# The planner of a fused attention, MoE and soft-MoE kernel: earlier ready times for first products, and new counted matmul durations

## The chip, the core and the metric

One core of one Trainium2 chip runs the kernel. The metric is the device time of one execution in microseconds (us); smaller is better. The engines are TensorE (PE, with its weight loads as PEld), VectorE (DVE), ScalarE (ACT), GpSimd (POOL) and SyncE (SP, which issues the DMAs).

## What is computed

Attention with pooled keys and values, then a feed-forward pair with h·cos(h), then eight experts over all tokens, weighted by a matrix that is normalised by rows and columns eight times:

```python
def _moe_ref(x, w_in, w_out):                      # 2304 tokens, 512 -> 2048 -> 512
    h = x @ w_in
    return (h * np.cos(h)) @ w_out

def _moe2_ref(x, w_gate, w1, w2):                  # 8 experts, 512 -> 1024 -> 512
    ...
    for e in range(E):
        h = np.maximum(x @ w1[e], 0.0)
        out += P[:, e:e + 1] * (h @ w2[e])
    return out.astype(np.float32)
```

## The kernel before, in words

All matrix products are of fp32r halves: each operand is cut into a high and a low part, and three matmuls stand for one product (high·high, high·low, low·high). The experts' stage, from about 500 us to the end, is 16 units (8 experts, two halves of the hidden width) by 3 pairs of 384-token blocks: 48 steps. In each step two layers are multiplied by a seven-product scheme (P1 to P7, taken in the order P1 P5 P6 P2 P7 P3 P4). `first_layer` does it twice (h = 0, 1), in matmuls of 384 columns, six to a product: P1 goes into PSUM tile px1, ACT copies it into tile py, P5 goes into pv5, P6 is added into py, P2 into px1, P7 into py, P3 into pv5, P4 into py. `strassen_layer` does it for three row blocks i, in matmuls of 256 columns, six to a product. A PSUM tile p (trace name pc) and a tile q (qc) each hold 512 columns, in two halves p0, p1, q0, q1. Products come in pairs of twelve matmuls, one node of the planner each: P1 into p0 and P5 into p1; P6 into q0 and P2 into p0; P7 into q0 and P3 into p1; last P4 alone into q0. Between them ACT copies p0 to q0 and p1 to s5 (trace name t), DVE adds q0 and s5 into p1 and later s5 into q1 (trace: qc<-qc,t), and `accumulate` (L1550) adds p and q into the output.

Weights of a unit come in as tiles raw (or raw2 for the second layer); DVE or POOL combine them (raw<-raw,raw, 128x2x256), ACT makes the high half (whi, vhi), DVE or POOL the low half (wlo, vlo). `VG` gives such an operation to whichever of the two the planner finds earlier.

The order of the work on each engine is set by a planner, `Graph.schedule`. Every piece of work is a node with an engine and a duration (`mm` counts those of PE). `latest` (L207) walks back from the goals and gives each node a time `late` that ranks it. `schedule` keeps a clock for each engine and picks the ready node that can start within a short hold of the earliest and has the smallest `late`. When a node has run, its followers get their ready time:

```python
s.est = max(s.est, end + (0.35 * lap if same else self.SIGNAL[e] + s.pad))
```

`pad` is an extra of the follower, 0.0 unless set. The planner's times set the order alone; the waits that the built program has come from the tiles which an instruction reads and writes. Each engine then runs its own list in order. The line numbers of the profile are those of the code below.

Of the kernel before, what the change touches and what calls it, by code (L numbers as in the profile page):

```python
# [15 lines left out]
ALU = mybir.AluOpType  # L16
# [26 lines left out]
HD = DM // 2  # L43
# [109 lines left out]
class Graph:  # L153
# [19 lines left out]
    def buf(self, kind, shape, dtype, name):  # L173
        return Buf(kind, shape, dtype, name)
# [4 lines left out]
    def add(self, engine, us, run, reads=(), writes=(), port=False, table=None, size=0, goal=FAR, name=None, pad=0.0, release=0.0):  # L179
        node = Node()  # L180
        node.engine, node.us = (engine, us) if isinstance(engine, tuple) else ((engine,), (us,))
        node.run, node.port, node.table, node.size, node.goal = run, port, table, size, goal
        node.succ, node.new, node.bufs, node.done, node.est, node.name = [], [], [], False, release, name
        node.pad, node.spare, node.lap = pad, None, self.lap
        deps = set()
        for items, write in ((reads, False), (writes, True)):
            for item in items:
                buf, part = item if isinstance(item, tuple) else (item, None)
                if buf.kind and not buf.acc:
                    assert write, (name, buf.name)  # L190
                    node.new.append(buf)
                for other, its, wrote in buf.acc:
                    if other is not node and (write or wrote) and (part is None or its is None or part == its):
                        deps.add(other)
                buf.acc.append((node, part, write))
                if buf not in node.bufs:
                    node.bufs.append(buf)
                    buf.left += 1
                    if buf.kind:
                        for group in buf.kind.groups:  # L200
                            group.users += 1
        node.wait = len(deps)
        for other in deps:
            other.succ.append(node)
        self.nodes.append(node)
        return node

    def latest(self):
        for node in reversed(self.nodes):
            late = node.goal  # L210
            for s in node.succ:
                late = min(late, s.late - max(node.us) - self.SIGNAL[node.engine[0]])
            node.late = late
            if node.size:
                node.late -= 3.0 if node.engine == ("SP",) else 7.0
# [195 lines left out]
def two(n):  # L411
    return (n + 151) / 960
# [16 lines left out]


def mm(count, n):
    return count * {384: 0.1736, 256: 0.117, 512: 0.2325}[n]


def V(n, port=True):
    return {"engine": "V", "us": two(n), "port": port}
# [12 lines left out]
def fused_kernel(ctx: ExitStack, tc: tile.TileContext, qT, kT, kS, vS, v0, k1, v1, wa1, wb1, wa2, wb2, wg, out):  # L449
# [12 lines left out]
    late = g.group("late", "right", (early, turn), ahead)  # L462
# [75 lines left out]
    def activate(n, out, in_, func=AF.Copy, reads=(), writes=(), from_psum=False, table=None, us=None, goal=FAR, **more):  # L538
        return add("A", us or (actp if from_psum else act)(n),
                   lambda: nc.scalar.activation(out=out(), in_=in_(), func=func,  # L540
                                                **{k: v() if callable(v) else v for k, v in more.items()}),
                   reads, writes, table=table)
# [11 lines left out]
    def tt(how, out, in0, in1, op, reads, writes):  # L554

        def run(e=how["engine"]):
            (nc.gpsimd if e == "G" else nc.vector).tensor_tensor(out=out(), in0=in0(), in1=in1(), op=op)  # L557

        return add(how["engine"], how["us"], run, reads, writes, port=how.get("port", False))
# [13 lines left out]
    def pe(us, run, reads, writes, goal=None, pad=0.0, spare=None):  # L573

        if goal is None:
            goal = clock["t"]
            clock["t"] += us * clock["pace"]
        node = add("PE", us, run, reads, writes, goal=goal, pad=pad)
        node.spare = spare
        return node  # L580
# [412 lines left out]
    def hidden1(j, w, f, cut):  # L993

        hi, lo = xts[j]
        bank = buf(b_h, [P, 512], F32, "ph")
        ps = lambda: bank[:, :NB]
        wh, wl = w
        for part in ((0, 1), (2, 3)) if cut else ((0, 1, 2, 3),):
            pe(mm(3 * len(part), NB), lambda part=part: three(  # L1000
                ps(), NB, lambda c: (wh[:, c * P:(c + 1) * P], wl[:, c * P:(c + 1) * P]), lambda c: (hi[:, c, :], lo[:, c, :]),
                part, KC), [wh, wl] + [t.part(c) for t in (hi, lo) for c in part], [bank],
               spare=(lambda: bank[:, NB:]) if part[-1] == KC - 1 else None)
        return cosine(ps, bank)
# [529 lines left out]
    def accumulate(pair, u, j, i, po, acc2):  # L1534

        e = u // UE
        t = pair * 2 * TPB + j * TPB + i
        if j not in acc2:
            acc2[j] = buf(k_acc2[2 * pair + j], [P, TPB, DM], F32, "acc2")
        box = acc2[j]  # L1540
        a, pe_ = lambda: box[:, i, :], lambda: pr[:, t, e:e + 1]
        if e == 0:
            if u == 0:
                either(DM, a, lambda: po.tile, [po], [(box, i)])
            else:
                tt(V(DM, False), a, lambda: po.tile, a, ALU.add, [po], [(box, i)])
            if u == UE - 1:
                activate(DM, a, a, reads=[pr], writes=[(box, i)], scale=pe_)
        else:
            add("V", two(DM), lambda: nc.vector.scalar_tensor_tensor(  # L1550
                out=a(), in0=po.tile, scalar=pe_(), in1=a(), op0=ALU.mult, op1=ALU.add), [po, pr], [(box, i)])
        if u == NU - 1:
            load(lambda: out[t * P:(t + 1) * P, :], a, P * DM * 4, reads=[(box, i)])

    def strassen_layer(pair, u, pieces, w, acc2, goals, own=None):

        def mms(ps, name, i, start=False):
            r = slice(i * P, (i + 1) * P)
            for h in range(2):
                gh, gl = pieces[name, h]  # L1560
                k = slice(h * HD, (h + 1) * HD)
                for n, (l, m) in enumerate(((gh, w[name][0]), (gh, w[name][1]), (gl, w[name][0]))):
                    nc.tensor.matmul(out=ps, lhsT=l[:, r], rhs=m[:, k], start=(start and h + n == 0),  # L1563
                                     stop=(h + n == 3), skip_group_check=True)

        def needs(*names):
            return [t for n in names for h in range(2) for t in pieces[n, h]] + [t for n in names for t in w[n]]

        for i in range(TPB):
            kp, kq = (own or {}).get(i, (b_p, b_q))  # L1570
            p, q = buf(kp, [P, DM], F32, "pc"), buf(kq, [P, DM], F32, "qc")
            s5 = buf(k_t5, [P, HD], F32, "t5")
            p0, p1 = (lambda p=p: p[:, :HD]), (lambda p=p: p[:, HD:])
            q0, q1 = (lambda q=q: q[:, :HD]), (lambda q=q: q[:, HD:])

            def two_products(a, an, b, bn, start=False, i=i):
                def run():
                    mms(a(), an, i, start)
                    mms(b(), bn, i)
                return run  # L1580

            pe(mm(12, HD), two_products(p0, "P1", p1, "P5", True), needs("P1", "P5"), [p], goal=goals[i][0])
            activate(HD, q0, p0, reads=[p], writes=[q], from_psum=True)
            activate(HD, lambda s5=s5: s5.tile, p1, reads=[p], writes=[s5], from_psum=True)
            pe(mm(12, HD), two_products(q0, "P6", p0, "P2"), needs("P6", "P2"), [p, q], goal=goals[i][1])
            tt(V(HD, False), p1, q0, lambda s5=s5: s5.tile, ALU.add, [q, s5], [p])
            pe(mm(12, HD), two_products(q0, "P7", p1, "P3"), needs("P7", "P3"), [p, q], goal=goals[i][2])
            tt(V(HD, False), q1, q0, lambda s5=s5: s5.tile, ALU.add, [s5], [q])
            accumulate(pair, u, 0, i, p, acc2)
            pe(mm(6, HD), lambda i=i, q0=q0: mms(q0(), "P4", i), needs("P4"), [q], goal=goals[i][3])  # L1590
            accumulate(pair, u, 1, i, q, acc2)
# [103 lines left out]
```

## Time and profile before

| | us |
|---|---|
| device time, median of 3 runs (lowest, highest) | 1903.47 (1903.32, 1905.5) |
| device time of the profiled execution | 1907.59 |
| its span, first to last instruction | 1905.9 |
| PE busy, share of the span | 1889.6, 99% |
| PE weight loads | 1853.0, 97% |
| DVE / ACT / POOL busy | 1504.0 / 1102.6 / 360.7 |
| mean granted TensorE clock | 0.998 |

"Busy" is the time in which an engine has an instruction under way. Matmuls overlap, each being recorded for longer than the distance to the next one, so the distance from one start to the next tells the pace and a wait shows as a longer distance. In timeline rows the columns are start, duration, engine, line, operation, output<-inputs, shape, count, and in brackets the idle time before it and who ended it.

### The profile page before, as it was taken

Reading aid. Unit: us, or ns where it says so; the run is one execution under the profiler, and the core shown is the slowest. Engines: PE = TensorE matmul, PEld = TensorE weight load, DVE = VectorE, ACT = ScalarE, POOL = GpSimd, SP = SyncE. Lnnn points to the kernel's source line nnn. Section 1 sums busy time; section 2 is a strip of 40 time slices with the busy share of each in tenths; the row PEclk is TensorE's granted clock in tenths of the full one; section 3 lists DMA queues with packets and bytes.
Section 4 is the critical chain, followed back from the end, with each engine's and each line's share of the span. In section 5 each row is a group of like instructions: output and inputs, shape, how many; then the busy total and the mean of one; then the engine's idle time right before and its main releaser. Section 6 shows DMA issues by size and latency. Waiting matters only on the chain.

```text
span 1905.9 us, 33965 instructions
## 1 busy us (share of the span) xinstructions
PE 1889.6 (99%) x13032; PEld 1853.0 (97%) x13032; DVE 1504.0 (79%) x2721; ACT 1102.6 (58%) x2375; POOL 360.7 (19%) x260
## 2 busy tenths in 40 slices
PE   9999999999999999999999999999999999999999
PEld 7789998899999999999999999999999999999998
DVE  7998856987787787778787787877877877878776
ACT  5865434675566665555555565555555565655653
POOL 0213332242102021212122121212121120212120
PEclk9999999999999999999999999999999999999999
DMA  8856662577656556556456465565465564655653
GB/s 267 245 187 238 239 169 71 188 256 263 232 224 254 202 202 262 187 210 243 185 208 257 155 250 212 191 261 198 196 243 194 199 265 160 244 221 191 235 217 116
DMA packets 104762, 406.76 MB, mean 213 GB/s; under 512 B 11160, under 2 KB 15896, under 8 KB 102552
## 3 DMA queue, kind: packets, MB, share of 16 engines
q1 hardware_dynamic: 102616, 400.01, 56.2%
q0 software_dynamic: 1984, 4.59, 1.4%
q8 instruction: 102, 1.67, 0.3%
q14 instruction: 60, 0.49, 0.1%
HBM read 363.40 MB, written 41.16 MB: 212 GB/s over the span
## 4 chain that ended last, share of the span: by engine, by line
PE 93%; DVE 4%; ACT 2%; DMA 1%; issue 0%; SPq 0%; ACTq 0%; DVEq 0%
PE pc L1563 20%; PE py L1178 17%; PE qc L1563 16%; PE px L1178 11%; PE pv L1178 11%; PE po L989 3%; PE po L990 3%; PE po L991 3%; PE ph L989 2%; PE ph L990 2%; PE ph L991 2%; PE px L897 1%; PE ptr L883 0%; DMA wc<-wac 0%; DVE xd L557 0%
## 5 line engine op out<-in xcount | busy, mean ns | idle before, releaser
L1563 PE MATMUL pc<-vlo,gh 128*128 128x256 f32 x1152 | 318.0, 276 | 0.0
L1563 PE MATMUL pc<-vhi,gl 128*128 128x256 f32 x1152 | 318.0, 276 | 0.0
L1563 PE MATMUL pc<-vhi,gh 128*128 128x256 f32 x1152 | 318.0, 276 | 0.0
L1178 PE MATMUL py<-xc,whi 128*128 128x384 f32 x1152 | 293.7, 335 | 0.0
L557 DVE TENSOR_TENSOR gl<-sf,gh 128x384 fp32r<-128x384 f32 x384 | 228.4, 624 | 29.4 <-ACT gh L540 29.2
L540 ACT ACTIVATE gh<-sf 128x384 fp32r<-128x384 f32 x384 | 194.8, 524 | 93.6 <-DVE sf L557 91.5
L1563 PE MATMUL qc<-vhi,gh 128*128 128x256 f32 x864 | 241.7, 280 | 0.9 <-DVE qc L557 0.5
L1563 PE MATMUL qc<-vlo,gh 128*128 128x256 f32 x864 | 239.0, 277 | 0.0
L1563 PE MATMUL qc<-vhi,gl 128*128 128x256 f32 x864 | 238.9, 276 | 0.0
L557 POOL TENSOR_TENSOR raw<-raw 128x512 f32<-128x512 f32 x46 | 60.1, 1307 | 930.3 <-DVE wlo L557 584.4
L1563 PEld LDWEIGHTS pc<-vhi,gh 128*128 128x128 f32 x1152 | 216.3, 188 | 0.1
L1563 PEld LDWEIGHTS pc<-vhi,gl 128*128 128x128 f32 x1152 | 216.3, 188 | 0.0
L1563 PEld LDWEIGHTS pc<-vlo,gh 128*128 128x128 f32 x1152 | 216.2, 188 | 0.0
L1178 PEld LDWEIGHTS py<-xc,whi 128*128 128x128 f32 x1152 | 199.3, 188 | 0.9 <-ACT py L540 0.6
L1178 PE MATMUL px<-xc,whi 128*128 128x384 f32 x768 | 196.5, 336 | 0.0
L1178 PE MATMUL pv<-xc,whi 128*128 128x384 f32 x768 | 196.1, 336 | 0.0
L1178 PE MATMUL py<-xc,wlo 128*128 128x384 f32 x576 | 192.5, 334 | 0.0
L1563 PEld LDWEIGHTS qc<-vhi,gh 128*128 128x128 f32 x864 | 162.1, 188 | 4.6 <-DVE qc L557 0.9
L1563 PEld LDWEIGHTS qc<-vhi,gl 128*128 128x128 f32 x864 | 162.4, 188 | 0.0
L1563 PEld LDWEIGHTS qc<-vlo,gh 128*128 128x128 f32 x864 | 162.1, 188 | 0.0
L1178 PEld LDWEIGHTS px<-xc,whi 128*128 128x128 f32 x768 | 130.1, 188 | 0.6 <-issue 0.6
L1178 PEld LDWEIGHTS pv<-xc,whi 128*128 128x128 f32 x768 | 130.3, 188 | 0.0
(245 smaller groups left out, 4578.6 us busy)
## 6 DMA issues: line engine op xcount, KB each, us to landing
xc<-xc SPq DMA_DIRECT2D x357, 768.0 KB, 6.7
wc<-wac SPq DMA_DIRECT2D x112, 256.0 KB, 4.6
raw<-wb SPq DMA_DIRECT2D x32, 512.0 KB, 7.8
raw<-wa SPq DMA_DIRECT2D x32, 512.0 KB, 4.7
raw<-wa SPq DMA_DIRECT2D x8, 1024.0 KB, 7.2
raw<-wb SPq DMA_DIRECT2D x8, 1024.0 KB, 6.2
wac<-m SPq DMA_DIRECT2D x12, 512.0 KB, 6.3
wac<-cw SPq DMA_DIRECT2D x12, 512.0 KB, 3.7
```

The source lines that it names most:

```text
L540: lambda: nc.scalar.activation(out=out(), in_=in_(), func=func, **{k: v() if callable(v) else v for k, v in more.items()}),
L557: (nc.gpsimd if e == "G" else nc.vector).tensor_tensor(out=out(), in0=in0(), in1=in1(), op=op)
L897: nc.tensor.matmul(out=bank[e * D:(e + 1) * D, off:off + n], lhsT=vs[b][:, 2 * hp + e, :], rhs=pt[:, 2 * hh + e, off:off + n], start=(off ...
L989: nc.tensor.matmul(out=ps, lhsT=lh, rhs=rh, start=(i == 0), stop=False)
L990: nc.tensor.matmul(out=ps, lhsT=lh, rhs=rl, start=False, stop=False)
L991: nc.tensor.matmul(out=ps, lhsT=ll, rhs=rh, start=False, stop=(i == total - 1))
L1178: nc.tensor.matmul(out=ps(), lhsT=l[:, k], rhs=r[:, c, :], start=(start and c + n == 0), stop=(c + n == 3), skip_group_check=True)
L1563: nc.tensor.matmul(out=ps, lhsT=l[:, r], rhs=m[:, k], start=(start and h + n == 0), stop=(h + n == 3), skip_group_check=True)
```

## The change

Three things in the planner, and nothing in what is computed. `strassen_layer` gets a constant `LEAD`, minus six matmuls of 256 columns, and sets it as `pad` on three followers of a pair: ACT's copy of p0 to q0, DVE's sum into p1, and DVE's sum into q1. Their ready time is put 0.68 us ahead. `latest` takes the negative pad into account. `mm` counts 256 columns with 0.1134 us in place of 0.117 us, and 384 columns with 0.1737 in place of 0.1736.

```diff
         for node in reversed(self.nodes):
             late = node.goal
             for s in node.succ:
-                late = min(late, s.late - max(node.us) - self.SIGNAL[node.engine[0]])
+                late = min(late, s.late - max(node.us) - self.SIGNAL[node.engine[0]] - min(0.0, s.pad))
...
 def mm(count, n):
-    return count * {384: 0.1736, 256: 0.117, 512: 0.2325}[n]
+    return count * {384: 0.1737, 256: 0.1134, 512: 0.2325}[n]
...
     def strassen_layer(pair, u, pieces, w, acc2, goals, own=None):
+        LEAD = -mm(6, HD)
...
             pe(mm(12, HD), two_products(p0, "P1", p1, "P5", True), needs("P1", "P5"), [p], goal=goals[i][0])
-            activate(HD, q0, p0, reads=[p], writes=[q], from_psum=True)
+            activate(HD, q0, p0, reads=[p], writes=[q], from_psum=True).pad = LEAD
             activate(HD, lambda s5=s5: s5.tile, p1, reads=[p], writes=[s5], from_psum=True)
             pe(mm(12, HD), two_products(q0, "P6", p0, "P2"), needs("P6", "P2"), [p, q], goal=goals[i][1])
-            tt(V(HD, False), p1, q0, lambda s5=s5: s5.tile, ALU.add, [q, s5], [p])
+            tt(V(HD, False), p1, q0, lambda s5=s5: s5.tile, ALU.add, [q, s5], [p]).pad = LEAD
             pe(mm(12, HD), two_products(q0, "P7", p1, "P3"), needs("P7", "P3"), [p, q], goal=goals[i][2])
-            tt(V(HD, False), q1, q0, lambda s5=s5: s5.tile, ALU.add, [s5], [q])
+            tt(V(HD, False), q1, q0, lambda s5=s5: s5.tile, ALU.add, [s5], [q]).pad = LEAD
```

PE's 12,761 matmuls are the same in both programs, in another order. Until about 157 us of the trace PE's order is the same; between there and 530 us it differs in two short pieces; after that it differs in each unit. DVE and POOL exchange work: of the 48 combinations raw<-raw,raw one was DVE's before and 17 are now, and POOL takes 61 of the vlo halves where it took 44.

The following places lie in the second half of one unit of the experts' stage (near 1044 us of the trace before); the pattern returns in 13 of the 16 units.

**PE, first layer, P1 (px) to P6 (py).** Before, P4 of a row block (qc) stands between P1 and P5 (pv); five more rows of pv follow, then P6 in py:

```order
L1178 MATMUL px_12434<-xc,whi 128x384 x2
L1178 MATMUL px_12434<-xc,wlo 128x384
L1178 MATMUL px_12434<-xc,whi 128x384 x2
L1178 MATMUL px_12434<-xc,wlo 128x384
L1563 MATMUL qc<-vhi,gh 128x256
L1563 MATMUL qc<-vlo,gh 128x256
L1563 MATMUL qc<-vhi,gl 128x256
L1563 MATMUL qc<-vhi,gh 128x256
L1563 MATMUL qc<-vlo,gh 128x256
L1563 MATMUL qc<-vhi,gl 128x256
L1178 MATMUL pv_12459<-xc,whi 128x384 x2
```

Now:

```order
L1178 MATMUL px_12448<-xc,whi 128x384 x2
L1178 MATMUL px_12448<-xc,wlo 128x384
L1178 MATMUL px_12448<-xc,whi 128x384 x2
L1178 MATMUL px_12448<-xc,wlo 128x384
L1178 MATMUL pv_12463<-xc,whi 128x384 x2
L1178 MATMUL pv_12463<-xc,wlo 128x384
L1178 MATMUL pv_12463<-xc,whi 128x384 x2
L1178 MATMUL pv_12463<-xc,wlo 128x384
L1178 MATMUL py<-xc,whi 128x384 x2
```

The qc group has moved to just ahead of px, so that only P5 stands between P1 and P6.

**ACT, around the copy of P1 (py<-px1).** Before, and now:

```order
L540 ACTIVATE vhi_12419<-raw2_12062 128x512
L540 ACTIVATE gh_12430<-c22_12381 128x384
L540 ACTIVATE sf_12443<-py_12300 128x384
L540 ACTIVATE vhi_12446<-raw2_12086 128x512
L540 ACTIVATE py_12456<-px1_12434 128x384
```

```order
L540 ACTIVATE vhi_12433<-raw2_12084 128x512
L540 ACTIVATE sf_12445<-py_12307 128x384
L540 ACTIVATE gh_12455<-sf_12445 128x384
L540 ACTIVATE vhi_12460<-raw2_12103 128x512
L540 ACTIVATE py_12470<-px1_12448 128x384
```

In both, a vhi made from a combined weight tile stands right ahead of the copy. The tile is raw2_12086 before and raw2_12103 now, and these are POOL's rows on it, before and now:

```order
L557 TENSOR_TENSOR raw2_12086<-raw2_12086 128x2x256
L557 TENSOR_TENSOR raw2_12086<-raw2_12062,raw2_12086 128x2x256 x2
L557 TENSOR_TENSOR vlo_12420<-raw2_12062,vhi_12419 128x512
L557 TENSOR_TENSOR vlo_12472<-raw2_12062,vhi_12471 128x512
L557 TENSOR_TENSOR raw2_12062<-raw2_12062,raw2_12086 128x2x256
```

```order
L557 TENSOR_TENSOR raw2_12103<-raw2_12103 128x2x256
L557 TENSOR_TENSOR raw2_12103<-raw2_12084,raw2_12103 128x2x256
L557 TENSOR_TENSOR vlo_12399<-raw2_12084,vhi_12398 128x512
L557 TENSOR_TENSOR vlo_12434<-raw2_12084,vhi_12433 128x512
L557 TENSOR_TENSOR vlo_12473<-raw2_12103,vhi_12472 128x512
L557 TENSOR_TENSOR raw2_12084<-raw2_12084,raw2_12103 128x2x256
```

The second raw2<-raw2_…,raw2 combination has left POOL; a vlo on the other tile (vlo_12434) stands in its time.

**DVE, from the vlo ahead of it to the sum of P6 (pv5<-py, which P7 waits for).** Before, and now:

```order
L557 TENSOR_TENSOR vlo_12396<-raw2_12086,vhi_12395 128x512
L1550 SCALAR_TENSOR_TENSOR acc2_6686<-pc_12320,pr_5725,acc2_6686 128x512
L557 TENSOR_TENSOR qc_12342<-qc_12342,t5_12344 128x256
L557 TENSOR_TENSOR gl_12379<-sf_12273,gh_12378 128x384
L557 TENSOR_TENSOR gl_12417<-spare_5467,gh_12416 128x384
L557 TENSOR_TENSOR gl_12384<-sf_12270,gh_12383 128x384
L1550 SCALAR_TENSOR_TENSOR acc2_6706<-qc_12342,pr_5725,acc2_6706 128x512
L557 TENSOR_TENSOR sf_12273<-sf_12270,sf_12273 128x384
L557 TENSOR_TENSOR pv5_12459<-py_12456,s5_12480 128x384
```

```order
L557 TENSOR_TENSOR qc_12336<-qc_12336,t5_12344 128x256
L1550 SCALAR_TENSOR_TENSOR acc2_6682<-pc_12320,pr_5725,acc2_6682 128x512
L557 TENSOR_TENSOR vlo_12396<-raw2_12103,vhi_12395 128x512
L557 TENSOR_TENSOR raw2_12103<-raw2_12084,raw2_12103 128x2x256
L1550 SCALAR_TENSOR_TENSOR acc2_6705<-qc_12336,pr_5725,acc2_6705 128x512
L557 TENSOR_TENSOR gl_12379<-sf_12305,gh_12378 128x384
L557 TENSOR_TENSOR sf_12305<-sf_12264,sf_12305 128x384
L557 TENSOR_TENSOR gl_12384<-spare_5467,gh_12383 128x384
L557 TENSOR_TENSOR gl_12421<-spare_5467,gh_12420 128x384
L557 TENSOR_TENSOR sf_12496<-spare_5467 128x384
L557 TENSOR_TENSOR vlo_12461<-raw2_12103,vhi_12460 128x512
L557 TENSOR_TENSOR pv5_12463<-py_12470,s5_12482 128x384
```

The sum qc<-qc,t now stands ahead of the accumulation of p (L1550), as it does in all 144 row blocks, where it stood behind in 135. The combination raw2_12103 stands behind vlo_12396, and ahead of pv5 there are four rows on SBUF tiles (gl, gl, sf, vlo) where three such rows stood further up before.

## Rows read from the trace of the kernel before

**Rows 1.** Busy time of each engine in two stretches, with granted clock.

```profile
core 0: us, PE busy (x) PEld busy (x) DVE busy (x) ACT busy (x) POOL busy (x), PEclk, DMA share, GB/s
296.00:303.00 7.00, 5.06 (x21) 4.74 (x20) 5.24 (x9) 2.41 (x5) 2.26 (x2) 0.76 0.01 4
600.00:1870.00 1270.00, 1270.00 (x9193) 1267.01 (x9193) 997.82 (x1822) 732.79 (x1628) 222.09 (x159) 1.00 0.56 216
```

**Rows 2.** Timeline of PE at 712 us and at 1843 us.

```profile
711.89 0.28 PE L1563 MATMUL pc<-vhi,gl 128*128 128x256 f32 x1
712.08 0.36 PE L1563 MATMUL qc<-vhi,gh 128*128 128x256 f32 x1
712.27 0.28 PE L1563 MATMUL qc<-vlo,gh 128*128 128x256 f32 x1
...
1843.89 0.36 PE L1563 MATMUL qc<-vhi,gh 128*128 128x256 f32 x1
```

**Rows 3.** Timeline of DVE at 711 us.

```profile
710.84 0.75 DVE L1550 SCALAR_TENSOR_TENSOR acc<-pc,pr,acc 128x512 f32<-128x512 f32 x1 [0.64 <-PE pc L1563]
711.51 0.42 DVE L557 TENSOR_TENSOR qc<-qc,t 128x256 f32<-128x256 f32 x1
```

**Rows 4.** Timeline of PE at 576 us and at the end.

```profile
576.70 0.34 PE L1178 MATMUL pv<-xc,wlo 128*128 128x384 f32 x1
577.42 0.39 PE L1563 MATMUL qc<-vhi,gh 128*128 128x256 f32 x1 [0.38 <-DVE pc L557]
577.65 0.29 PE L1563 MATMUL qc<-vlo,gh 128*128 128x256 f32 x1
...
1899.97 0.28 PE L1563 MATMUL qc<-vhi,gl 128*128 128x256 f32 x1
1900.75 0.38 PE L1563 MATMUL qc<-vhi,gh 128*128 128x256 f32 x1 [0.50 <-DVE qc L557]
```

**Rows 5.** Timeline of PE and ACT around one pair P1, P5 (twelve matmuls).

```profile
1007.07 0.28 PE L1563 MATMUL pc<-vhi,gh 128*128 128x256 f32 x1
...
1008.32 0.28 PE L1563 MATMUL pc<-vhi,gl 128*128 128x256 f32 x1
1008.43 0.52 PE L1178 MATMUL px<-xc,whi 128*128 128x384 f32 x2
1008.63 0.37 ACT L540 ACTIVATE qc<-pc 128x256 f32<-128x256 f32 x1 [0.29 <-PE pc L1563]
```

**Rows 6.** Timeline of POOL, then DVE, at 1015 us.

```profile
1015.36 1.30 POOL L557 TENSOR_TENSOR wlo<-raw,whi 128x512 fp32r<-128x512 f32 x1 [1.79 <-ACT whi L540]
1015.71 1.36 DVE L557 TENSOR_TENSOR gl<-sf,gh 128x384 fp32r<-128x384 f32 x1
1016.99 0.55 DVE L557 TENSOR_TENSOR gl<-spare,gh 128x384 fp32r<-128x384 f32 x1
```

**Rows 7.** Timeline of POOL, PE, ACT and DVE around P1, P6 and P7.

```profile
1043.84 1.29 POOL L557 TENSOR_TENSOR raw<-raw,raw 128x512 f32<-128x512 f32 x1 [1.62 <-DVE vlo L557]
1044.23 0.51 PE L1178 MATMUL px<-xc,whi 128*128 128x384 f32 x2
1045.17 0.63 ACT L540 ACTIVATE vhi<-raw 128x512 fp32r<-128x512 f32 x1 [0.20 <-POOL raw L557]
1045.71 0.47 ACT L540 ACTIVATE py<-px 128x384 f32<-128x384 f32 x1
1047.00 0.51 PE L1178 MATMUL py<-xc,whi 128*128 128x384 f32 x2
...
1049.12 0.55 DVE L557 TENSOR_TENSOR pv<-py,s 128x384 f32<-128x384 f32 x1
1050.44 0.51 PE L1178 MATMUL py<-xc,whi 128*128 128x384 f32 x2
```

**Rows 8.** Groups by line and shape: ACT's and POOL's share of vhi and vlo.

```profile
L540 ACT ACTIVATE vhi<-raw 128x512 fp32r<-128x512 f32 x112 | 69.8, 624 | 4.0 <-POOL raw L557 3.0 <-PE pv L1178 0.9
L557 POOL TENSOR_TENSOR vlo<-raw,vhi 128x512 fp32r<-128x512 f32 x44 | 69.2, 1573 | 102.8 <-ACT vhi L540 95.9 <-PE pv L1178 6.9
```

## The prediction

> **What bounds the kernel now.** First the busy shares by stretch, since a mean over the span would hide stages. From 600 to 1870 us PE is busy in 1270.00 of 1270.00 us at a granted clock of 1.00, DVE in 79%, ACT in 58%, POOL in 17% [rows 1]. Busy is not yet at pace, because matmuls overlap; so next come the starts of neighbouring matmuls. Twelve of 256 columns take 1008.43 − 1007.07 = 1.36 us [rows 5], 0.1134 us a slot. P1 to P6 in the first layer is 2.77 us; without the six slots of 256 columns between them that leaves 0.174 us for each of twelve of 384 [rows 7]. Almost every slot of the experts' stage has these lengths. As the matmuls are the same in both programs, the change can win only the few longer gaps, and can lose by making new ones. From the same P4 in one unit to that in the unit 13 later the time is (1843.89 − 712.08)/13 = 87.06 us [rows 2]: the figure that the change moves.
>
> **What there is to win.** (a) At the P4 of a row block two distances in a row are 0.19 us instead of 0.113 [rows 2]: 0.15 us. The cause stands beside it: DVE runs acc<-pc first, then qc<-qc,t, which ends at 711.93, and P4, which needs that sum, follows at 712.08 [rows 3]. A second P4 of the unit loses one such distance by the same order: I take 0.24 us a unit (bounds 0.15 and 0.30), over 14 units 3.4 us. The new order has the sum ahead of the accumulation in all 144 row blocks, so all of it goes. (b) At 576 us PE waits 577.42 − 576.70 − 0.17 = 0.55 us for DVE's pc and loses 0.11 more at the restart; the last P4 waits 1900.75 − 1899.97 − 0.11 = 0.67 and about 0.1 more [rows 4]. Both are of this kind: 1.4 us. (c) At 296 us PE is busy in 5.06 of 7.00 us and the clock falls to 0.76 on average [rows 1]; the order there is unchanged, so it stays. Together −4.8 us.
>
> **The change part by part.** The constants of `mm` and the term in `latest` add no instruction; they only re-sort. The three pads say that a follower may begin when the first product of a pair has ended. In the trace ACT's copy qc<-pc waits until 1008.63, which is 0.20 us after the slot of the twelfth matmul (0.29 us idle, ended by PE pc) [rows 5]: it waits for P5, not for P1. DVE's sum into p1 shares tile p with P2 in the same way. Only the sum into q1, which has tile q, can follow P7 before P3 ends. For two of the three followers, then, the planner believes in 0.68 us that the program doesn't give. The Trainium skill (PSUM — Partial Sum Buffer, "PSUM bank collisions raise a hardware error") says the same against this change: two engines may not touch one bank at once and waits are to be set by bank, so a copy of p0 beside P5's writes into p1 could not be had at all; this trace agrees, with its 0.20 us after the pair.
>
> Neighbouring edits that only swap copies, gh and gl are costed at nothing: ACT and DVE are idle for 42% and 21% of the stage [rows 1], and the consumers are products later. If that cover is gone, one late copy costs PE its length, 0.47 us [rows 7]. DMA issues keep their number, and no weight is late in the stage before. The stage before 530 us changes in two short pieces: 0, ±1 us. The first, irregular unit of the new pattern I charge with nothing. Two moves have no such cover; both come in 13 units.
>
> **Move A, P6 loses the qc group ahead of it.** Clock 0 is P1's first matmul. Before, P6 was due at 2.77 (1.04 for P1, 0.68 for qc, 1.04 for P5), now at 2.09. What it needs is ACT's py copy, which stands behind the vhi of the combined weight. That combination is now DVE's, behind acc<-pc and vlo.
> - PE: the qc group (0.68) and a py product (1.04) now stand between the P3 pair and clock 0, so the pair ends at −1.72. DVE's acc starts 0.20 later, at −1.52, and takes 0.75 [rows 3]; vlo is wider than the 0.55 of a 384-column gl [rows 6], about 0.63. DVE asks for the combination at about −0.1.
> - POOL's vlo_12434 waits for vhi_12433. ACT makes that after the gh copies and ahead of sf, which can start at −0.48 (py product ends at −0.68, plus 0.20). POOL so asks at about −0.3, ahead of DVE by 0.2.
> - What happens when DVE reads two SBUF operands while POOL reads its own: gl took 1.36 us instead of 0.55 and ended 0.41 after POOL's wlo [rows 6]. So POOL runs to about 1.05 (1.30 long), and DVE's combination ends at 1.5.
> - ACT's vhi, 0.62 [rows 8], and the copy, 0.47 [rows 7], with their handovers: 2.65. P6 is late by 0.56, plus 0.1 for the restart [rows 2]: **0.7 us**. Before, the same copy began at 1.48 on this clock and was done 0.8 us before it was due [rows 7].
>
> Bounds: 0 (DVE asks first, ends near 0.6, all done by 1.8) and 1.0 (vhi_12433 another 0.4 late). I take 0.7, since the asks follow from waits that PE sets.
>
> The Trainium skill (SBUF — State Buffer, "Who interferes with whom") gives the rule: a DVE instruction with two SBUF inputs contends with a POOL instruction that reads SBUF, and whoever issues first holds the port while the other is fully blocked. The trace agrees as far as 1.36 against 0.55 us goes; by the rule the whole of A hangs on the 0.2 us between the two requests.
>
> **Move B, the sum that P7 needs.** Clock 0 is P6. P7 is due at 1.04 + 1.04 + 1.36 + 1.36 = 4.81 (P6, P2, two pairs). Before it was 3.44 [rows 7]; one pair more lies between now, but DVE's queue ahead of the sum has grown by more. After the combination it has acc, gl, sf, gl (0.67 from start to start for acc [rows 3], 0.47 to 0.55 for the others) from −1.24 to about 1.0. Then come gl, sf and vlo on SBUF while POOL runs vlo_12473 (its vhi is ready at 0.5; alone 1.30, on the mean 1.57 [rows 6, 8]) and right behind it raw2_12084 (1.29 [rows 7]). The first gl is blocked to POOL's end at 2.3 plus 0.41 = 2.7; the sf behind it to POOL's second end, 4.0 + 0.41 = 4.4; vlo 0.6; pv's sum 0.55 [rows 7], which ends at 5.5. Late by 0.7, plus 0.1: **0.8 us**. Bounds: 0 (POOL's two rows don't both fall on DVE's) and 1.1 (POOL's own rows are stretched to their mean).
>
> **Sum.** 13 × (0.7 + 0.8) = 19.5, minus 4.8: +14.7 us. A unit grows by 1.5 − 0.24 to 88.3 us. The profiled execution, 1907.59 us, would become 1922.3. It is 4.1 us above the median of the runs; the difference carried over, the prediction against the median 1903.47 is **1918.2 us**. With A from 0.5 to 0.9 and B from 0.5 to 1.0 this case reaches from 1911.7 to 1923.4.
>
> **Rivals.**
> - *Neither wait bites; faster.* The place is the same port. If DVE's combination asks before POOL's vlo, it ends 0.9 us sooner, the copy is in time, POOL comes later and DVE's queue is through before P7. It decides at the 0.2 us between the two requests. For it: 0.2 is small against two chains of four steps. Against it: both chains start from PE, so they repeat alike in each unit. Then −4.8 remains: 1898.7 us.
> - *One of the two bites.* A delay at A shifts PE against DVE and POOL by 0.7, so B may dissolve, or A may be in time and B not: 13 × 0.75 − 4.8 = +5: 1908.5 us.
> - *More bites.* A further SBUF pair meets POOL's 61 vlo halves, another 0.5 us a unit: 1924.7 us or more.
> - *The change doesn't do what it says.* That is my reading of two pads, and part of the forecast. If the copies did start after the first product, ACT and DVE would run 0.68 us sooner, both waits would vanish, and the time would be near 1898.7 too.
>
> **How the numbers follow.** About 0.2% of the time, 3.8 us, can be told from no change. Chances: both waits 0.54, one 0.16, none (with the pads at their word) 0.20, more 0.06, something early in the kernel 0.04. "None" is 4.8 us faster, just past the bound: 0.17 faster, 0.03 same. "One" lies just past it on the other side: 0.10 slower, 0.06 same. The rest of 0.04 is 0.01 faster, 0.03 same. Faster 0.18, same 0.12, slower 0.70. The range takes in "none" (1898.7), "one" and both waits with their bounds, and leaves out "more": 1898 to 1924.
>
> **What would show it.** Right: PE waits for ACT's py copy at P6 and for DVE's pv sum at P7, some 13 each, of 0.5 to 0.8 us; DVE's raw<-raw,raw at 1.6 us where it has POOL beside it; the 0.19 us pairs at P4 gone; a unit of 88.3 us; a clock still at 1.00, since the waits of 0.55 and 0.67 stand among matmuls of the usual length [rows 4]. ACT's qc<-pc still starts 0.2 us after the pair. Wrong: a unit of 86.9 us or less, with DVE's combination near 0.6 us; or qc<-pc starting inside the pair; or waits on other products.

## Result and the profile after

The changed kernel takes 1916.8 us (median of 6 runs, 1915.43 to 1919.84) beside 1903.86 us before (6 runs): ratio 1.0068, 95% interval 1.0055 to 1.0081, so 12.9 us slower (10.5 to 15.4). The prediction was 1918.2 us, slower.

First the busy shares of the stage from 600 to 1870 us after the change, columns as in [rows 1]:

```profile
600.00:1870.00 1270.00, 1260.23 (x9092) 1252.03 (x9092) 995.56 (x1803) 723.50 (x1614) 217.52 (x161) 1.00 0.56 214
```

PE, which had no idle time there in [rows 1], now has 9.8 us of it, at the same clock of 1.00. The window holds less of the work now (9092 of PE's rows instead of 9193), so DVE's slightly smaller busy time there says nothing. Over the whole execution DVE is busy for 1511.9 us instead of 1504.0 with one row less (2720 instead of 2721), so rows of DVE have become longer. The view of PE's waits says where the idle time lies from 600 us on (engine and line, what it waited for: us in total, times, longest):

```profile
PE py L1178 <- ACT py L540: 5.1, 13, 0.4
PE py L1178 <- DVE pv L557: 4.4, 14, 0.6
PE px L1178 <- DMA xc<-xc: 0.2, 1, 0.2
PE qc L1565 <- DVE qc L557: 0.2, 1, 0.2
```

The first two rows are P6 and P7 of the first layer. The view counts only time in which no matmul is open; what a wait costs is read from the starts. The timeline of PE around P6 and P7 of one unit, and P6 of the unit 12 later:

```profile
782.50 0.52 PE L1178 MATMUL px<-xc,whi 128*128 128x384 f32 x2
...
784.41 0.34 PE L1178 MATMUL pv<-xc,wlo 128*128 128x384 f32 x1
785.14 0.62 PE L1178 MATMUL py<-xc,whi 128*128 128x384 f32 x2 [0.39 <-ACT py L540]
785.60 0.33 PE L1178 MATMUL py<-xc,wlo 128*128 128x384 f32 x1
...
789.94 0.28 PE L1565 MATMUL pc<-vhi,gl 128*128 128x256 f32 x1
790.51 0.62 PE L1178 MATMUL py<-xc,whi 128*128 128x384 f32 x2 [0.30 <-DVE pv L557]
...
1840.77 0.62 PE L1178 MATMUL py<-xc,whi 128*128 128x384 f32 x2 [0.39 <-ACT py L540]
```

P6 starts 785.14 − 784.41 − 0.17 = 0.55 us late, and its first two matmuls take 0.46 us instead of 0.35: 0.66 in all. P7 is late by 790.51 − 789.94 − 0.11 = 0.46, and with the same 0.11 loses 0.57. A unit takes (1840.77 − 785.14)/12 = 87.97 us, where it took 87.06 [rows 2].

Why P6 is late stands in the timelines of POOL, DVE and ACT just ahead of it:

```profile
782.19 1.30 POOL L557 TENSOR_TENSOR vlo<-raw,vhi 128x512 fp32r<-128x512 f32 x1 [1.10 <-ACT vhi L540]
782.36 1.68 DVE L557 TENSOR_TENSOR raw<-raw,raw 128x512 f32<-128x512 f32 x1
784.07 0.63 ACT L540 ACTIVATE vhi<-raw 128x512 fp32r<-128x512 f32 x1 [1.01 <-DVE raw L557]
784.61 0.47 ACT L540 ACTIVATE py<-px 128x384 f32<-128x384 f32 x1
```

POOL begins 0.17 us ahead of DVE. DVE's combination then takes 1.68 us and ends at 784.04, 0.55 after POOL; ACT's vhi and, behind it, the copy that P6 needs follow at once. The timelines of POOL and DVE between P6 and P7:

```profile
785.71 1.68 POOL L557 TENSOR_TENSOR vlo<-raw,vhi 128x512 fp32r<-128x512 f32 x1 [2.22 <-ACT vhi L540]
787.36 1.60 POOL L557 TENSOR_TENSOR raw<-raw,raw 128x512 f32<-128x512 f32 x1
785.68 2.13 DVE L557 TENSOR_TENSOR gl<-spare,gh 128x384 fp32r<-128x384 f32 x2
787.74 1.64 DVE L557 TENSOR_TENSOR sf<-spare 128x384 f32<-128x384 f32 x1
789.30 0.68 DVE L557 TENSOR_TENSOR vlo<-raw,vhi 128x512 fp32r<-128x512 f32 x1
789.90 0.55 DVE L557 TENSOR_TENSOR pv<-py,s 128x384 f32<-128x384 f32 x1
```

Two gl rows take 2.13 us and one sf 1.64, where 0.55 each is usual [rows 6]; the sum that P7 needs ends at 790.45. Last, ACT's copy in a place where it had nothing else to do: the pair's first matmul, what follows its twelve, and the copy:

```profile
815.78 0.28 PE L1565 MATMUL pc<-vhi,gh 128*128 128x256 f32 x1
...
817.14 0.52 PE L1178 MATMUL px<-xc,whi 128*128 128x384 f32 x2
817.34 0.37 ACT L540 ACTIVATE qc<-pc 128x256 f32<-128x256 f32 x1 [0.77 <-PE pc L1565]
```

It still starts 0.20 us after the whole pair, as in [rows 5]. DVE's sum into p1 does the same, 0.20 us after the slot of the pair's last matmul (820.47 + 0.11):

```profile
820.47 0.28 PE L1565 MATMUL pc<-vhi,gl 128*128 128x256 f32 x1
820.78 0.43 DVE L557 TENSOR_TENSOR pc<-qc,t 128x256 f32<-128x256 f32 x1 [0.47 <-PE pc L1565]
```

For these two followers the ready time that the planner now takes does not come about. The sum into q1 does get it: one starts at 780.29 us, 0.20 us after P7's slot and 0.48 us ahead of the end of the pair's last slot.

### The profile page after: what moved, and what is told of

Read it like the earlier page. It is cut to its first block, busy times and chain, and to the rows that moved or that the text cites. A ratio compares the mean times of both kernels' runs of the same rounds, so it can differ in the third digit from the quotient of the medians.

```text
span 1915.8 us, 33914 instructions
## 1 busy us (share of the span) xinstructions
PE 1891.6 (99%) x13032; PEld 1850.2 (97%) x13032; DVE 1511.9 (79%) x2720; ACT 1098.1 (57%) x2372; POOL 360.3 (19%) x264
## 3 DMA queue, kind: packets, MB, share of 16 engines
q8 instruction: 102, 1.67, 0.4%
## 4 chain that ended last, share of the span: by engine, by line
PE 85%; DVE 9%; issue 2%; DMA 2%; ACT 2%; SPq 0%; POOL 0%; POOLq 0%; DVEq 0%; ACTq 0%
PE pc L1565 18%; PE py L1178 15%; PE qc L1565 15%; PE pv L1178 10%; PE px L1178 10%; PE po L989 3%; PE po L991 3%; PE po L990 3%; PE ph L989 2%; PE ph L991 2%; PE ph L990 2%; DVE sf L557 2%; DVE raw L557 1%; DVE gl L557 1%; DVE vlo L557 1%
## 5 line engine op out<-in xcount | busy, mean ns | idle before, releaser
L557 DVE TENSOR_TENSOR gl<-sf,gh 128x384 fp32r<-128x384 f32 x384 | 204.0, 561 | 31.8 <-ACT gh L540 31.6
L540 ACT ACTIVATE qc<-pc 128x256 f32<-128x256 f32 x144 | 53.1, 369 | 136.7 <-PE pc L1565 136.6
```

## Experiments

The theory has two parts. What costs time is DVE and POOL reading SBUF operands at once, ahead of an ACT copy and a DVE sum that PE waits for (*port*); what brings that about is the order that the pads make. The rivals: a chain that is too long whatever POOL does; the two pads that the program doesn't keep as the whole cause; the counted durations.

**Which part of the change makes the order.** Four variants ran together, with 1903.56 us for the kernel before.

e1, the counts alone:

```diff
-    return count * {384: 0.1736, 256: 0.117, 512: 0.2325}[n]
+    return count * {384: 0.1737, 256: 0.1134, 512: 0.2325}[n]
```

> The two new counted durations alone (0.1134 and 0.1737 us), no pads. Theory: the loss comes from the pads' order, and the counts alone remove the P4 waits of 0.24 us a unit; PE waits for nothing between 600 and 1870 us, a unit takes 86.8 us, and the time is 3 to 4 us under that of before: 1900 (1899 to 1902). Rival, any tighter order loses: waits at P6 or P7 of the first layer come here too, 1908 or more.

1902.58 us, ratio 0.9993 (0.9984 to 1.0001). From 600 to 1870 us not even the weight loads pause any more:

```profile
600.00:1870.00 1270.00, 1270.00 (x9231) 1270.00 (x9230) 999.76 (x1831) 733.74 (x1631) 216.01 (x157) 1.00 0.57 216
```

So the counts do remove the gaps at P4 and bring no new wait there, and the rival falls. The regular unit takes 86.71 us, beside 86.8 expected. But the time came out 2.6 us above the expected point and 0.6 above the range, and its interval does not exclude no change. Part of that is a wait ahead of the window that the kernel before doesn't have. It costs 0.83 us by the starts, restart included, where the wait at 576 us, which is gone, cost 0.66 [rows 4]:

```profile
581.52 0.61 PE L1178 MATMUL px<-xc,whi 128*128 128x384 f32 x2 [0.56 <-ACT py L540]
```

The last P4 waits as before. e9 and e11 come back to the rest.

e2, the pads alone (the change with the count of 256 columns back at 0.117 and of 384 at 0.1736). `LEAD` follows the count and is 0.70 us here.

> The three pads and the term in latest, with the old counted durations 0.117 and 0.1736. Theory: the pads alone make the order that loses; 13 waits each at P6 (for ACT's py copy) and P7 (for DVE's pv sum), about 1917 (1913 to 1921). Rival, the counts are needed for it, as they are what makes the planner's clock run ahead: no such waits, within 3 us of 1903.9.

1917.47 us, ratio 1.0076 (1.0063 to 1.0088), with the waits of the whole change:

```profile
PE py L1178 <- ACT py L540: 5.5, 14, 0.4
PE py L1178 <- DVE pv L557: 3.9, 14, 0.3
```

The pads make the order that loses, with either count.

e3, the counts and only the third pad:

```diff
-            activate(HD, q0, p0, reads=[p], writes=[q], from_psum=True).pad = LEAD
+            activate(HD, q0, p0, reads=[p], writes=[q], from_psum=True)
...
-            tt(V(HD, False), p1, q0, lambda s5=s5: s5.tile, ALU.add, [q, s5], [p]).pad = LEAD
+            tt(V(HD, False), p1, q0, lambda s5=s5: s5.tile, ALU.add, [q, s5], [p])
```

> New counts and only the pad on the sum into q1, the one whose ready time the program keeps. Theory A, the two pads that the program doesn't keep are the whole cause: waits gone, 1900 (1898 to 1903). Theory B, a tighter order that lets DVE and POOL meet on SBUF operands is the cause, whether the pad is true or not: the waits move to other products, some 0.3 to 0.5 us each in the 13 units, 1907 to 1913.

1911.71 us, ratio 1.0047 (1.0034 to 1.006): theory B. The one wait of the regular units that the view shows, and the timelines of POOL and DVE ahead of it:

```profile
PE pc L1565 <- DVE gl L557: 2.9, 14, 0.2
```

```profile
782.90 1.55 POOL L557 TENSOR_TENSOR vlo<-raw,vhi 128x512 fp32r<-128x512 f32 x1 [0.57 <-ACT vhi L540]
784.41 1.61 POOL L557 TENSOR_TENSOR raw<-raw,raw 128x512 f32<-128x512 f32 x1
783.20 1.67 DVE L557 TENSOR_TENSOR gl<-sf,gh 128x384 fp32r<-128x384 f32 x1
784.79 1.64 DVE L557 TENSOR_TENSOR gl<-spare,gh 128x384 fp32r<-128x384 f32 x1
```

The same pair of POOL rows now meets two gl rows that a pair of the second layer needs. A pad that the program keeps is no protection.

e4, the counts and only the first two pads (`.pad = LEAD` taken off the sum into q1).

> New counts and only the pads on ACT's copy of p0 and on DVE's sum into p1, which the program makes wait for the pair's end. Theory A: as slow as the whole change, 1916 to 1920. Theory B, with the planner 0.68 us wrong and the true sum no longer pulled ahead: waits behind the accumulation come back beside the port's, slower than the whole change, 1920 to 1935. If neither, and the pads do no harm: 1900 to 1905.

1937.27 us, ratio 1.0178 (1.0164 to 1.0192), 2 us above even theory B's range. PE's waits, here over the whole execution:

```profile
PE py L1178 <- DVE pv L557: 8.6, 15, 0.7
PE pc L1565 <- DVE gl L557: 7.3, 14, 0.5
PE qc L1565 <- DVE qc L557: 3.8, 16, 0.5
```

All three kinds of wait stand side by side. So the two pads that aren't kept do the most harm alone, and the third, harmful with the counts alone, makes them cheaper: the effects don't add, since each setting is another order. That the waits of e3 and e4 come from the port is read from timelines like the one above; no run takes POOL's rows away in these two orders.

**Whether the port is the cause at P6 and P7.** These keep the changed order on every engine and change only what POOL does at the two meetings of each unit. They ran together with e8, with 1904.79 us for the kernel before. e5 replaces POOL's subtraction for P3's low half; what is left out by it stands in the expectation.

```diff
+            if name in SHORT:                      # ('P3',)
+                node, x, lo, hi = g.nodes[-1], what[1], parts[1], parts[0]
+
+                def run(e):
+                    if e == "G":
+                        return nc.gpsimd.memset(lo.tile.bitcast(F32), 0.0)
...
+                node.run = run
```

> The whole change, its order on every engine kept, but POOL writes zeros into the vlo of P3's weights (the one beside DVE's combination) instead of subtracting: it then reads nothing from SBUF there. Theory port: DVE's combination takes 0.7 us instead of 1.68, the 13 waits for ACT's py copy at P6 (0.55 us and 0.11 for the restart each, 8.6 us in all) go; DVE's queue behind it is 0.9 us earlier, so the waits at P7 shrink or stay: 1902 to 1909. Rival, ACT's and DVE's chain is too long for a P6 that is due 0.68 us sooner, whatever POOL does: all waits stay, 1915 to 1919.

1903.18 us, ratio 0.9994 (0.9984 to 1.0004). The timelines of POOL, DVE and ACT at the same place:

```profile
779.97 0.53 POOL L1417 MEMSET vlo<- 128x512 f32 x1
781.28 0.69 DVE L557 TENSOR_TENSOR raw<-raw,raw 128x512 f32<-128x512 f32 x1
782.01 0.63 ACT L540 ACTIVATE vhi<-raw 128x512 fp32r<-128x512 f32 x1
782.67 0.47 ACT L540 ACTIVATE py<-px 128x384 f32<-128x384 f32 x1
```

POOL is done before DVE begins, and DVE's combination takes 0.69 us instead of 1.68. The view shows no wait at P6 or P7 any more, and DVE's queue runs earlier by what the combination saved. By the starts P6 is on time, but P7 is not quite: DVE's gl and sf ahead of it are still blocked (2.14 us for two and 1.65). The timeline of PE at P7:

```profile
788.20 0.28 PE L1575 MATMUL pc<-vhi,gl 128*128 128x256 f32 x1
788.44 0.62 PE L1178 MATMUL py<-xc,whi 128*128 128x384 f32 x2
```

P7 is 788.44 − 788.20 − 0.11 = 0.13 us late and loses 0.11 more at its restart, about 3 us in 13 units.

e6 does the same to P7's low half, and lets POOL's combination for P4 work on 32 of 256 columns:

```diff
+            if name in SHORT:                      # ('P7',), as in e5
...
         combine(b21, b21, b11)
+        node = g.nodes[-1]
+
+        def run(e):
+            c = CUT if e == "G" else HD            # 32
...
+                out=b21[1]()[:, :, :c], in0=b21[1]()[:, :, :c], in1=b11[1]()[:, :, :c], op=ALU.subtract)
+
+        node.run = run
```

> The same order; POOL writes zeros into the vlo of P7's weights, and its combination for P4's weights takes 32 of 256 columns: the two POOL rows beside DVE's gl and sf. Theory port: gl and sf take 0.55 us each instead of 1.6, the waits for DVE's pv at P7 (0.46 and 0.11 each, 7.4 us in all) go, those at P6 stay: 1909 (1907 to 1911). Rival, DVE's queue is simply too long ahead of pv: they stay, 1915 to 1919.

1907.03 us, ratio 1.0009 (0.9997 to 1.0021), 2 us under its point and at the edge of its range. PE's waits from 600 us on:

```profile
PE py L1178 <- ACT py L540: 5.1, 13, 0.4
PE qc L1583 <- DVE qc L557: 0.2, 1, 0.2
```

```profile
783.09 1.02 DVE L557 TENSOR_TENSOR gl<-spare,gh 128x384 fp32r<-128x384 f32 x2
784.03 0.55 DVE L557 TENSOR_TENSOR sf<-spare 128x384 f32<-128x384 f32 x1
```

The waits at P6 stand as they were, those at P7 are gone, and gl and sf have their usual length in DVE's timeline.

e7 joins e5 and e6.

> Both of these in one. Theory port: no waits of PE in the regular units, a unit near 86.8 us, 1901 (1899 to 1904), below before. Rival: 1915 to 1919; if a third thing adds its share, between the two.

1899.34 us, ratio 0.9979 (0.9968 to 0.999), with no PE wait in the regular units, which take 86.69 us. Against the changed kernel that is 17 us by the ratios, though PE's order is the very one that lost: the order costs nothing without the meetings. The rival of a chain that is too long falls.

These three runs shorten POOL's rows as well, so by themselves they don't tell a shared port from any other cost of two engines running at once. Two places in the traces do. In e7 a DVE row with two SBUF inputs starts while POOL is still writing zeros (POOL's two writes run until 786.10), and in the changed kernel a DVE row with one input in PSUM (py) lies wholly inside a POOL row that reads SBUF:

```profile
785.11 0.99 POOL L1417 MEMSET vlo<- 128x512 f32 x2
785.70 0.68 DVE L557 TENSOR_TENSOR vlo<-raw,vhi 128x512 fp32r<-128x512 f32 x1
```

```profile
777.15 1.30 POOL L557 TENSOR_TENSOR raw<-raw 128x512 f32<-128x512 f32 x1 [21.80 <-DVE vlo L557]
777.56 0.55 DVE L557 TENSOR_TENSOR c<-py,s 128x384 f32<-128x384 f32 x1
```

Both DVE rows have their usual length, 0.68 and 0.55 us; the first one's place returns in 13 units of e7 at 0.68 us each. In the changed kernel, by contrast, the 14 combinations raw<-raw,raw that meet a POOL row take 1.67 to 1.69 us each. Of the meetings shown here, DVE is held up only where its row has two SBUF inputs and POOL's row reads SBUF too.

**The term in `latest`.** e8 is the change with that line as before.

```diff
-                late = min(late, s.late - max(node.us) - self.SIGNAL[node.engine[0]] - min(0.0, s.pad))
+                late = min(late, s.late - max(node.us) - self.SIGNAL[node.engine[0]])
```

> The change without the term in latest: the pads shift the ready times alone and not the ranks. Theory, the pads act through the ready times: both waits stay, 1914 to 1919. Rival, half of the order comes from the ranks: read by the same steps its order keeps the meeting at P6 (0.66 us in 13 units) and loses the one at P7, 1906 to 1910.

1907.85 us, ratio 1.002 (1.001 to 1.003): the rival. The view of waits has "py <- ACT py" 14 times and none for DVE's pv. The meeting at P6 comes from the ready times, that at P7 needs the ranks.

**What the shift of 4 us was.** e9 is the kernel before, unchanged.

> The kernel before, unchanged, for a second profile. The prediction took the first one's 1907.59 us, 4 us above the median of the runs, as a fixed shift. Theory shift: this profile too is near 1907 and shows the wait of 2.1 us at 296 us with the lower granted clock behind it. Rival, the wait at 296 us varies from one execution to the next: a shorter wait there, the clock at 1.00, and 1902 to 1905; the unit between 712 and 1844 us stays at 87.06 us in both cases.

1903.43 us. The first row is the stretch from 296 us, the other two are the same two P4 as in [rows 2]:

```profile
296.00:303.00 7.00, 6.88 (x42) 6.00 (x43) 3.93 (x9) 2.45 (x5) 1.02 (x1) 1.00 0.01 2
```

```profile
708.38 0.36 PE L1563 MATMUL qc<-vhi,gh 128*128 128x256 f32 x1
...
1839.69 0.36 PE L1563 MATMUL qc<-vhi,gh 128*128 128x256 f32 x1
```

The window cuts the wait, which now begins ahead of 296 us; the timelines of PE show it whole, in the first profile of before and in e9:

```profile
298.31 0.44 PE L989 MATMUL po<-gh,wc 128*128 128x384 f32 x1 [1.94 <-DVE acc L557]
```

```profile
296.12 0.44 PE L989 MATMUL po<-gh,wc 128*128 128x384 f32 x1 [0.58 <-DVE acc L557]
```

The wait is 0.58 us instead of 1.94, the clock is 1.00 instead of 0.76, and the first P4 comes 3.7 us earlier. The 13 units take 1131.31 us beside 1131.81. The shift was a matter of that one execution, and 3.7 of its 4.2 us lay ahead of the experts' regular units.

**A version that beats both.** e10 counts 256 columns with 0.1134, leaves 384 at 0.1736, and sets the one true pad in the last unit alone, where no later unit's POOL work can meet it:

```diff
+            tt(V(HD, False), q1, q0, lambda s5=s5: s5.tile, ALU.add, [s5], [q]).pad = LEAD if u == NU - 1 else 0.0
```

> 0.1134 us counted for 256 columns, 0.1736 left for 384, and the one true pad (the sum into q1) in the last of the 16 units alone. Theory: no wait of PE between 600 us and the end, the last P4's 0.67 us gone too, a unit of 86.7 us: 4 us under before, 1899.5 (1898 to 1902). Rival, what the stage wins is given back in the stage before 530 us, whose order the counts move as well: within 1.5 us of before.

1901.9 us beside 1904.43, ratio 0.9979 (0.997 to 0.9989): by the ratio 4 us faster than before (2.1 to 5.7), and 17 faster than the change; the medians lie 2.5 us apart. From 600 us to the end PE waits for nothing, the tail included. The wait for ACT's py that e1 has near 580 us is here too.

e11 is e10 without the pad.

> 0.1134 us counted for 256 columns alone, no pads, 0.1736 left. Theory: this is the part of the two counts that acts, 3 us under before, 1900.5 (1899 to 1902.5). Rival: as with both counts, about 1 us under before.

1901.03 us, ratio 0.9988 (0.9979 to 0.9997). Alone the count of 256 columns gives 2.3 us (0.6 to 4) by the ratio, and its last P4 still waits 0.5 us by the view. By the time neither e1 nor e10 can be told from it: the intervals overlap. The profiles, one for each kernel, help: the table takes the experts' stage by itself, from the three matmuls of 512 columns into pset (L1149), which stand ahead of its first products, to the last matmul.

| run | matmuls into pset start, us | last matmul starts, us | between, us |
|---|---|---|---|
| before, first profile | 502.79 | 1901.42 | 1398.63 |
| before, second profile (e9) | 499.06 | 1897.25 | 1398.19 |
| the change | 500.98 | 1911.34 | 1410.36 |
| e1 | 501.13 | 1895.87 | 1394.74 |
| e11 | 499.58 | 1894.37 | 1394.79 |
| e10 | 502.09 | 1895.58 | 1393.49 |
| e7 | 506.03 | 1898.76 | 1392.73 |

In the stage e1 and e11 win 3.7 and 3.6 us against the mean of the two profiles of before, much as expected of them (3 to 4, and 3), so an effect of the count of 384 columns doesn't show there; e10 wins 4.9. Much of what blurs the times lies ahead of the stage: its start varies by 7 us over these profiles, and by 3.7 between the two of the kernel before.

## Why the prediction was right

**The mechanism and its two places held, step by step.** On the clock of move A (P1 at 782.50), POOL asked at −0.31 (forecast −0.3), DVE at −0.14 (−0.1), DVE's combination ended at 1.54 (1.5) and ACT's copy at 2.58 (2.65). P6 lost 0.66 us; 0.7 was forecast. e5 shows that the blocked combination was the cause, e6 and e7 the same for P7.

**Move B was a little too dear.** The term gave 0.8 and measured 0.57. On the clock of P6, the blocked sf ended at 4.24 (forecast 4.4), since POOL's second row ended at 3.82 (4.0), and pv's sum at 5.31 (5.5): 0.19 us sooner. Besides, P7 was due 0.11 us later than the 4.81 of the forecast, which left out P6's own restart. Against this, 0.06 us passed between the end of the sum and P7. The unit is 87.97 us, not 88.3.

**The gaps that were counted went, and a little more.** From 600 us on PE waits for DVE's qc once, for 0.2 us, in the first unit. The wait at 576 us and that of the last P4 are gone. The unit without waits is 86.69 us in e7 and 86.71 in e1, where 87.06 − 0.24 = 86.82 was counted: about 0.1 us a unit came on top.

**One term was left out: the first, irregular unit.** It was charged with nothing and has waits of its own, the largest at a P7, in PE's timeline:

```profile
701.24 0.62 PE L1178 MATMUL py<-xc,whi 128*128 128x384 f32 x2 [0.56 <-DVE pv L557]
```

Read by starts, this P7 and its restart cost 0.94 us, a P4 at 693 us 0.45, a P6 0.25: 1.6 us. With it the sum is 13 × (0.66 + 0.57) + 1.6 − 4.8 = 12.8 us, beside 12.9 measured (10.5 to 15.4). That the forecast of +14.7 lay only 1.8 us too high is thus in part luck, two errors of size that partly cancel: 3.5 us too much in move B and the roundings of A, 1.6 too little in the first unit. The sum's closeness to 12.9 isn't evidence either: the further 0.1 us a unit takes about 1.5 us off it, and by the profiles the stage is 11.7 to 12.2 us longer than before.

**Carrying the 4.1 us over was wrong as a reason.** I took the distance of the profiled execution to the median as a property of the kernel, and the wait at 296 us as fixed because the order there is unchanged. e9 shows that both vary between executions. It did no harm, since only the difference was added to the median.

**The rivals.** "Neither wait bites" fell; e7 bears out its price, −4.8 us (by the ratio −4.0, between −1.9 and −6.1). That DVE's combination asks first at P6 was not tried by itself. "One of the two bites" fell for the change, but is what e8 does: by the ratio 3.8 us slower than before (1.9 to 5.7), beside the +5 that it was priced at. "The change doesn't do what it says" holds for two pads, as forecast (copy and sum into p1 each 0.20 us after the pair). But I made more of that than it bears: e3, with the true pad alone and the counts, is 8 us slower than before. A kernel in which the copy may begin after P1, with P5 in another bank, was not tried.

## What to carry to other kernels

When PE has no slack, a re-sorted order is judged by what meets on the other engines in each repeat, and not by whether the planner's durations became truer: here truer counts alone won 3.7 us in the experts' stage (e1, e11; 1 to 2 us of the whole time, where e1's interval still takes in none), and the same counts with a truer ready time lost 8 in the whole time. Look for two-operand SBUF work of DVE beside POOL's ahead of anything that PE waits for, and price it at POOL's end plus about half a microsecond. Take a second profile of the kernel before, before a fixed wait or an offset enters a sum.

## What the runs showed of the hardware that was not expected

Where both engines have several such rows, they take turns. At 785.68 us DVE's gl began 0.03 us ahead of POOL's vlo: POOL's row grew to 1.68 us from 1.30, the second gl ended 0.42 us after it, POOL's next row grew to 1.60, and sf ended 0.42 us after that. So the cost falls on both, and e7, without these meetings, has POOL's other rows of these two kinds at 1.30 to 1.32 us in the mean. The Trainium skill (SBUF — State Buffer, "Who interferes with whom") says that who issues first holds the port for a whole instruction; this trace agrees at both places, with POOL 0.17 us ahead at P6 and DVE 0.03 us ahead here. The blocked row ended 0.42 us after POOL's with 384 columns and 0.55 with 512. A POOL row that only writes held up nothing (e7), nor was a DVE row with an input in PSUM held up.

The wait at 296 us differs between executions: 1.94 us of idle time and a granted clock of 0.76 in the first profile of before, 0.58 us and 1.00 in the second. After the change PE waits 27 times at P6 and P7, for about half a microsecond each, and the clock stays at 1.00.
